# Retention and two feed-forward blocks: the moving operands of the four large products read as two interleaved halves

## The chip, the cores and the metric

The kernel runs on one core of a Trainium2 chip. The metric is the device time of one execution in microseconds (us). The engines are PE (TensorE: matmuls; its weight loads are listed as PEld), DVE (VectorE), ACT (ScalarE), POOL (GpSimd) and SP (SyncE, which issues the DMAs).

## The reference

```python
def _attn_ref(q, k, v):                       # (4, 8, 768, 64) each
    gamma = 1.0 - 2.0 ** (-5.0 - np.arange(H))
    for t in range(S):
        state = gamma * state + outer(k[:, :, t], v[:, :, t])
        y[:, :, t] = scale * (q[:, :, t] @ state)

def _moe_ref(x, w_in, w_out):                 # x (3072, 512), w_in (512, 2048), w_out (2048, 512)
    h = x @ w_in
    return np.maximum(0.01 * h, h) @ w_out

def _moe2_ref(x, w_in, w_out):
    h = x @ w_in
    return (h - np.tanh(h)) @ w_out

# reference: y as (3072, 512), then _moe_ref, then _moe2_ref
```

The four large products are the two matrix products of each feed-forward block. The weights of the blocks come in 64-bit floats, which the kernel turns into 32-bit ones itself.

## The kernel before

Tokens are worked on in six blocks (`nb`, `NC` = 6) of 512: four batches of 128 tokens each. In the feed-forward blocks a tile is 128 partitions by 512 words of 32 bits; for activations the partitions are features and the 512 words are tokens.

**Retention** (lines 368 to 566) leaves x as tiles `xw`, features by tokens.

**First product** (`product`, L637 to L645). The token blocks are taken in pairs and the 2x2 blocks of x and `w_in` are multiplied by a scheme of seven products (Strassen's, in Winograd's form), 8 groups of them for each of the three pairs of blocks: 168 products. Each operand was split into an upper and a lower part (`xch`, `xcl`, `wg`); a product is 2 halves of the contraction times 3 matmuls (upper x upper, upper x lower, lower x upper). The moving operand is x. The sums go through `collect` and `rectify` into tiles `c` and to memory as `g1s`, features by tokens.

**Second product** (`mm_out1`, L595 to L613). For each of 96 tiles (6 blocks by 16 feature tiles) the tile `gr` is read back, split into `gh` and `gl` (ACT, then DVE), and multiplied: 4 output tiles times 3 matmuls. The moving operand is g, the stationary one the weights `wo`. After 16 feature tiles, four ACT copies `st` (L611) take the sums out of PSUM, and DMAs write them to `x2s`. The sums alternate between PSUM banks 0 to 3 and 4 to 7 from block to block.

**Third product** (`mm_l1`, L755). For each of 96 tiles: 4 contraction tiles times 3 matmuls. The moving operand is the split `xkh`, `xkl` of what `x2s` holds; the stationary one is `w2h`, `w2l` of `w_in` (half 0 of `W2`).

**Fourth product** (`mm_l2`, L768). For each of 96 tiles: 4 token groups times 3 matmuls. Here the stationary operand is the activation (`gh`, `gl`), and the moving one is the weight (half 1 of `W2`), so that the output comes out as tokens by features, is copied out by `evac` and written to `out`.

The weights of the second block are split by `second_weights` (L741 to L753) while the second product still runs; `el_1` and `el_2` compute h - tanh(h) and split it between the third and the fourth product, which alternate, the third being two tiles ahead.

The order of the instructions is written out by hand, with small generators that run in the background by a budget of microseconds; no scheduler moves anything. In each of the four products a matmul names a moving operand of 512 words in a row. The helper `split` (L143) is an ACT copy that rounds to the upper part and a subtraction for the lower one.

Of the kernel before, what the change touches and what calls it, by code (L numbers as in the profile page):

```python
# [9 lines left out]
F32 = mybir.dt.float32  # L10
# [4 lines left out]
AF = mybir.ActivationFunctionType  # L15
ALU = mybir.AluOpType
# [8 lines left out]
NK = DM // P  # L25
NM = DFF // P
# [45 lines left out]
def kernel(  # L72
# [12 lines left out]
    nc = tc.nc  # L85
# [20 lines left out]
    def alloc(nm, dt=F32, shape=(P, TB)):  # L106
        pool, tag = free.popleft()
        serial[0] += 1
        t = pool.tile(list(shape), dt, tag=tag, name=f"{nm}_{serial[0]}")
        home[id(t)] = (t, pool, tag)  # L110
        return t

    def give(*ts):
        for t in ts:
            _, pool, tag = home.pop(id(t))
            free.append((pool, tag))
# [26 lines left out]
    def split(hi, lo, src, eng):  # L143

        nc.scalar.activation(out=hi, in_=src, func=AF.Copy)  # L145
        eng.tensor_tensor(out=lo, in0=src, in1=hi.bitcast(F32), op=ALU.subtract)  # L146

    def upper(hi, src, scale=None):
        if scale is None:
            nc.scalar.activation(out=hi, in_=src, func=AF.Copy)  # L150
        else:
            nc.scalar.activation(out=hi, in_=src, func=AF.Copy, scale=scale)
# [423 lines left out]
    def bank(i, nm):  # L576
        return mp.tile([P, TB], F32, tag=f"b{i}", name=nm)
# [9 lines left out]
    G, ACC = {}, {}  # L587
# [7 lines left out]
    def mm_out1(n):  # L595
        nb, m = divmod(n, NM)
        if m == 0:
            for j in range(4):
                ACC[j] = bank((nb + 1) % 2 * 4 + j, f"o1_{nb}_{j}")
        g, w = G.pop(n), WO[m]  # L600
        for j in range(4):
            c = slice(j * P, (j + 1) * P)
            for i, (a, b) in enumerate(((w[0][:, c], g[0]), (w[0][:, c], g[1]), (w[1][:, c], g[0]))):
                nc.tensor.matmul(ACC[j], a, b, start=m == 0 and i == 0, stop=m == NM - 1 and i == 2)  # L604
        give(*g)
        if nb == NC - 1:
            give(*WO.pop(m))
        if m == NM - 1:
            for j in range(4):
                st = alloc("st")  # L610
                nc.scalar.activation(out=st, in_=ACC[j], func=AF.Copy)  # L611
                nc.sync.dma_start(out=x2s[nb, j], in_=st)
                give(st)  # L613

# [22 lines left out]
    def product(sb, g, nm):  # L637
        an, bn, bk, _ = PROD[nm]
        ps, first = get_bank(sb, g, bk)
        a, b = WG[g][0][an], XC[sb][bn]  # L640
        for kt in range(2):
            c = slice(kt * P, (kt + 1) * P)
            for i, (w, x) in enumerate(((a[0], b[kt][0]), (a[0], b[kt][1]), (a[1], b[kt][0]))):
                nc.tensor.matmul(ps, w[:, c], x, start=first and kt == 0 and i == 0, stop=kt == 1 and i == 2,  # L644
                                 skip_group_check=True)  # L645

    KEPT = {}
# [40 lines left out]
    for i, (at_, sb, g, nm) in enumerate(stream):  # L688
# [13 lines left out]
        if xleft:  # L702
            c, p = xleft.pop(0)
# [30 lines left out]
    W2 = {}  # L734

    def reload_w2(m):
        rl = cm.tile([P, 2, DM], F32, tag="raw", name=f"w2r_{m}", bufs=RAW_BUFS)
        nc.sync.dma_start(out=rl, in_=w2s[m])
        return rl

    def second_weights():  # L741
        rl = {0: reload_w2(0), 1: reload_w2(1)}
        for m in range(NM):
            if m + 2 < NM:
                rl[m + 2] = reload_w2(m + 2)
            while len(free) < 8:
                yield None
            W2[m] = []
            for half in range(2):
                W2[m].append((alloc("w2h", F32R), alloc("w2l", F32R)))  # L750
                split(*W2[m][half], rl[m][:, half], nc.vector)
                yield 0.7
            rl.pop(m)  # L753

    def mm_l1(n):  # L755
        nb, m = divmod(n, NM)
        h = bank(4 + n % 4, f"h_{n}")
        w = W2[m][0]
        for kt in range(NK):
            x = xk[nb, kt]  # L760
            c = slice(kt * P, (kt + 1) * P)
            for i, (a, b) in enumerate(((w[0][:, c], x[0]), (w[0][:, c], x[1]), (w[1][:, c], x[0]))):
                nc.tensor.matmul(h, a, b, start=kt == 0 and i == 0, stop=kt == NK - 1 and i == 2)  # L763
            if m == NM - 1:
                give(*x)
        H[n] = h

    def mm_l2(n):  # L768
        nb, m = divmod(n, NM)
        if m == 0:  # L770
            for j in range(4):
                ACC[j] = bank(j, f"acc_{nb}_{j}")
        g, w = G.pop(n), W2[m][1]
        for j in range(4):
            c = slice(j * P, (j + 1) * P)
            for i, (a, b) in enumerate(((g[0][:, c], w[0]), (g[0][:, c], w[1]), (g[1][:, c], w[0]))):
                nc.tensor.matmul(ACC[j], a, b, start=m == 0 and i == 0, stop=m == NM - 1 and i == 2)  # L777
        give(*g)

    def evac(n):  # L780
# [37 lines left out]
    for n in range(NT):  # L818
# [10 lines left out]
        nb, m = divmod(n, NM)  # L829
# [18 lines left out]
    for n in range(-LAG, NT):  # L848
        n1 = n + LAG
        if n1 < NT:  # L850
            nb, m = divmod(n1, NM)
# [71 lines left out]
```

## Time and profile before

| | |
|---|---|
| median of 3 runs | 1138.69 us (1138.53 to 1138.78) |
| span of the profiled execution | 1136.7 us |
| PE busy | 1126.8 us (99%) |
| DVE, ACT, POOL busy | 753.2, 594.1, 169.5 us |
| PE weight loads | 932.5 us, beside the matmuls |

The span runs from the first to the last instruction of the program in the one execution that was profiled; for that execution nothing but the span is given, and the median of the timed runs is 2.0 us above it. A matmul's busy time holds its way through the array, and the next one begins before it ends; how fast PE goes is therefore read from the distance between starts, or from the number of matmuls in a stretch in which PE was busy without a break.

### The profile page before, as it was taken

The numbers are of one execution on the slowest core, as the hardware profiler recorded it, in microseconds if no ns is written. First come the engines' busy times: TensorE is split into PE (matmuls) and PEld (weight loads), VectorE is DVE, ScalarE is ACT, GpSimd is POOL, SyncE is SP. The second block draws the span as 40 slices with busy tenths as digits, with TensorE's granted clock in tenths as the row PEclk, the third lists the DMA queues.
The fourth block names the chain that finished last, engine by engine and source line by source line (L and its number), as shares of the span: only waits on it lengthen the run. The fifth ranks groups of instructions, "written<-read, shape, count | busy, mean of one in ns | idle before, by whom it ended". The sixth has DMA issues, their size and how long they took to land.

```text
span 1136.7 us, 16464 instructions
## 1 busy us (share of the span) xinstructions
PE 1126.8 (99%) x6075; PEld 932.5 (82%) x6075; DVE 753.2 (66%) x1264; ACT 594.1 (52%) x1025; POOL 169.5 (15%) x156
## 2 busy tenths in 40 slices
PE   9999999999999999999999999999999999999998
PEld 6888788888888888888888888888888888888886
DVE  3578897656778566364464667677667667677665
ACT  5766677546666324333454445445455445445443
POOL 3230000000000000000001232232232232232221
PEclk9999999999999999999999999999999999999999
DMA  9995555774668676476562002002001000100000
GB/s 233 251 248 167 203 187 186 253 248 156 233 232 296 234 266 241 171 273 229 203 244 74 1 1 74 1 1 73 2 1 50 25 1 29 47 1 6 32 1 37
DMA packets 134449, 148.03 MB, mean 130 GB/s; under 512 B 57440, under 2 KB 86240, under 8 KB 134368
## 3 DMA queue, kind: packets, MB, share of 16 engines
q1 hardware_dynamic: 134080, 146.83, 38.8%
q8 instruction: 47, 0.77, 0.3%
q14 instruction: 34, 0.28, 0.1%
q10 hardware_dynamic: 288, 0.15, 0.0%
HBM read 96.61 MB, written 50.33 MB: 129 GB/s over the span
## 4 chain that ended last, share of the span: by engine, by line
PE 96%; DVE 2%; issue 1%; ACT 1%; DMA 0%; SPq 0%; DVEq 0%; ACTq 0%
PE acc L777 23%; PE h L763 23%; PE o L604 23%; PE X L644 11%; PE Y L644 5%; PE Z L644 3%; PE sc L489 2%; PE y L511 2%; PE y L507 2%; PE kTp L454 1%; PE qTp L468 1%; PE u L528 1%; DMA k<-in_k_dram 0%; ACT c L633 0%; DVE c L657 0%
## 5 line engine op out<-in xcount | busy, mean ns | idle before, releaser
L146 POOL TENSOR_TENSOR gl<-e,gh 128x512 fp32r<-128x512 f32 x95 | 122.7, 1292 | 878.1 <-ACT gh L145 822.2
L604 PE MATMUL o<-gh,wo 128*128 128x512 f32 x768 | 237.1, 389 | 0.0
L145 ACT ACTIVATE gh<-e 128x512 fp32r<-128x512 f32 x96 | 60.7, 633 | 220.2 <-DVE e L804 220.2
L604 PEld LDWEIGHTS o<-gh,wo 128*128 128x128 f32 x768 | 144.2, 188 | 30.0
L797 DVE SCALAR_TENSOR_TENSOR e<-e,h 128x512 f32<-128x512 f32 x96 | 66.0, 687 | 152.4 <-ACT e L795 152.4
L777 PE MATMUL acc<-w2h,gl 128*128 128x512 f32 x384 | 149.6, 390 | 0.0
L604 PE MATMUL o<-gl,wo 128*128 128x512 f32 x384 | 149.5, 389 | 0.1
L777 PE MATMUL acc<-w2h,gh 128*128 128x512 f32 x384 | 149.4, 389 | 0.0
L777 PE MATMUL acc<-w2l,gh 128*128 128x512 f32 x384 | 149.4, 389 | 0.0
L763 PE MATMUL h<-xkh,w2h 128*128 128x512 f32 x384 | 149.4, 389 | 0.0
L763 PE MATMUL h<-xkl,w2h 128*128 128x512 f32 x384 | 149.4, 389 | 0.0
L763 PE MATMUL h<-xkh,w2l 128*128 128x512 f32 x384 | 149.4, 389 | 0.0
L146 DVE TENSOR_TENSOR gl<-gr,gh 128x512 fp32r<-128x512 f32 x96 | 64.6, 686 | 98.8 <-ACT gh L145 97.3
L644 PE MATMUL X<-xch,wg 128*128 128x512 f32 x384 | 126.7, 390 | 1.3 <-DVE wg L156 1.3
L644 PEld LDWEIGHTS X<-xch,wg 128*128 128x128 f32 x384 | 71.9, 188 | 17.3 <-DVE wg L156 2.2
L777 PEld LDWEIGHTS acc<-w2h,gl 128*128 128x128 f32 x384 | 72.0, 188 | 15.7 <-DVE gl L146 0.4
L604 PEld LDWEIGHTS o<-gl,wo 128*128 128x128 f32 x384 | 72.1, 188 | 15.2 <-DVE gl L146 0.5
L777 PEld LDWEIGHTS acc<-w2h,gh 128*128 128x128 f32 x384 | 72.1, 188 | 15.1 <-ACT gh L145 0.2
L763 PEld LDWEIGHTS h<-xkl,w2h 128*128 128x128 f32 x384 | 72.1, 188 | 15.0
L763 PEld LDWEIGHTS h<-xkh,w2l 128*128 128x128 f32 x384 | 72.1, 188 | 14.9
L777 PEld LDWEIGHTS acc<-w2l,gh 128*128 128x128 f32 x384 | 72.1, 188 | 15.0
L763 PEld LDWEIGHTS h<-xkh,w2h 128*128 128x128 f32 x384 | 72.0, 188 | 14.8
(89 smaller groups left out, 1856.7 us busy)
## 6 DMA issues: line engine op xcount, KB each, us to landing
g1s<-c SPq DMA_DIRECT2D x96, 256.0 KB, 2.1
gr<-g1s SPq DMA_DIRECT2D x96, 256.0 KB, 4.8
raw<-in_moe_w_in_dram SPq DMA_DIRECT2D x32, 512.0 KB, 5.4
raw<-in_moe_w_out_dram SPq DMA_DIRECT2D x32, 512.0 KB, 4.4
w2s<-cv SPq DMA_DIRECT2D x32, 256.0 KB, 4.4
w2r<-w2s SPq DMA_DIRECT2D x16, 512.0 KB, 5.8
q<-in_q_dram SPq DMA_DIRECT2D x24, 256.0 KB, 4.0
k<-in_k_dram SPq DMA_DIRECT2D x48, 128.0 KB, 3.8
```

The lines of the kernel that those rows point to most:

```text
L145: nc.scalar.activation(out=hi, in_=src, func=AF.Copy)
L146: eng.tensor_tensor(out=lo, in0=src, in1=hi.bitcast(F32), op=ALU.subtract)
L454: nc.tensor.transpose(ps[:, b, :], d["k"][:, b].rearrange("p h d -> p (h d)"), ident)
L468: nc.tensor.transpose(ps[:, b, e, :], d["qp"][:, b2 + b, e].rearrange("p h d -> p (h d)"), ident)
L489: nc.tensor.matmul(sc[h][:, b, :], d["kT"][r, b, :], d["qT"][r, b, tq], start=True, stop=True)
L507: nc.tensor.matmul(y[r, b, :], U[p][r, b, :], d["qT"][r, b, tq], start=b == 0, stop=False)
L511: nc.tensor.matmul(y[r, b, :], d["v"][:, b, h, :], d["A"][h][:, b, :], start=c == 0 and b == 0, stop=b == NB - 1)
L604: nc.tensor.matmul(ACC[j], a, b, start=m == 0 and i == 0, stop=m == NM - 1 and i == 2)
L644: nc.tensor.matmul(ps, w[:, c], x, start=first and kt == 0 and i == 0, stop=kt == 1 and i == 2, skip_group_check=True)
L763: nc.tensor.matmul(h, a, b, start=kt == 0 and i == 0, stop=kt == NK - 1 and i == 2)
L777: nc.tensor.matmul(ACC[j], a, b, start=m == 0 and i == 0, stop=m == NM - 1 and i == 2)
L797: nc.vector.scalar_tensor_tensor(out=w, in0=u, scalar=C3, in1=h, op0=ALU.mult, op1=ALU.mult)
```

## The change

A new helper `il` gives a view of a tile of 512 words in which word 2b + a is word 256a + b of the tile: 0, 256, 1, 257, and so on. All moving operands of the four products go through it. As two neighbouring words of the view are 256 words apart, a matmul now reads its moving operand in steps of 1024 bytes forth and 1020 bytes back.

Each of the first three products so turns the order of its tokens once; three such turns make word 8b + a (a below 8, b below 64) out of 64a + b in one direction, and the reverse in the other. The four copies `st` behind the second product, where two turns are done, now read PSUM in steps of 8 words and write in a row, which puts the order so that the third product's turn gives the tokens their places again. In the fourth product the moving operand is a weight, so its columns are turned beforehand: the split of half 1 in `second_weights` reads in steps of 2 words and writes in a row, on ACT and DVE as before.

Built, both programs have the same instructions in the same order on every engine and on the same tiles; the access patterns named here differ, and 22 matmuls get one wait more. These are the first matmuls into a PSUM bank: 15 of the second product in blocks 2 to 5, 3 of the third (tiles 0 to 2) and 4 of the fourth (tile 0). Each now also waits on PE's own counter, for the matmuls that used its bank before. In the changed kernel the lines behind the helper are 4 to 13 higher.

```diff
--- before.py
+++ after.py
@@ -144,6 +144,10 @@
 
         nc.scalar.activation(out=hi, in_=src, func=AF.Copy)
         eng.tensor_tensor(out=lo, in0=src, in1=hi.bitcast(F32), op=ALU.subtract)
+
+    def il(x):
+
+        return x.rearrange("p (a b) -> p b a", a=2)
 
     def upper(hi, src, scale=None):
         if scale is None:
@@ -601,14 +605,15 @@
         for j in range(4):
             c = slice(j * P, (j + 1) * P)
             for i, (a, b) in enumerate(((w[0][:, c], g[0]), (w[0][:, c], g[1]), (w[1][:, c], g[0]))):
-                nc.tensor.matmul(ACC[j], a, b, start=m == 0 and i == 0, stop=m == NM - 1 and i == 2)
+                nc.tensor.matmul(ACC[j], a, il(b), start=m == 0 and i == 0, stop=m == NM - 1 and i == 2)
         give(*g)
         if nb == NC - 1:
             give(*WO.pop(m))
         if m == NM - 1:
             for j in range(4):
                 st = alloc("st")
-                nc.scalar.activation(out=st, in_=ACC[j], func=AF.Copy)
+                nc.scalar.activation(out=st.rearrange("p (a b) -> p a b", a=8),
+                                     in_=ACC[j].rearrange("p (b a) -> p a b", a=8), func=AF.Copy)
                 nc.sync.dma_start(out=x2s[nb, j], in_=st)
                 give(st)
 
@@ -641,7 +646,7 @@
         for kt in range(2):
             c = slice(kt * P, (kt + 1) * P)
             for i, (w, x) in enumerate(((a[0], b[kt][0]), (a[0], b[kt][1]), (a[1], b[kt][0]))):
-                nc.tensor.matmul(ps, w[:, c], x, start=first and kt == 0 and i == 0, stop=kt == 1 and i == 2,
+                nc.tensor.matmul(ps, w[:, c], il(x), start=first and kt == 0 and i == 0, stop=kt == 1 and i == 2,
                                  skip_group_check=True)
 
     KEPT = {}
@@ -748,7 +753,15 @@
             W2[m] = []
             for half in range(2):
                 W2[m].append((alloc("w2h", F32R), alloc("w2l", F32R)))
-                split(*W2[m][half], rl[m][:, half], nc.vector)
+                hi, lo = W2[m][half]
+                if half == 0:
+                    split(hi, lo, rl[m][:, 0], nc.vector)
+                else:
+                    src = rl[m][:, 1].rearrange("p (b a) -> p a b", a=2)
+                    nc.scalar.activation(out=hi.rearrange("p (a b) -> p a b", a=2), in_=src, func=AF.Copy)
+                    nc.vector.tensor_tensor(out=lo.rearrange("p (a b) -> p a b", a=2), in0=src,
+                                            in1=hi.rearrange("p (a b) -> p a b", a=2).bitcast(F32),
+                                            op=ALU.subtract)
                 yield 0.7
             rl.pop(m)
 
@@ -760,7 +773,7 @@
             x = xk[nb, kt]
             c = slice(kt * P, (kt + 1) * P)
             for i, (a, b) in enumerate(((w[0][:, c], x[0]), (w[0][:, c], x[1]), (w[1][:, c], x[0]))):
-                nc.tensor.matmul(h, a, b, start=kt == 0 and i == 0, stop=kt == NK - 1 and i == 2)
+                nc.tensor.matmul(h, a, il(b), start=kt == 0 and i == 0, stop=kt == NK - 1 and i == 2)
             if m == NM - 1:
                 give(*x)
         H[n] = h
@@ -774,7 +787,7 @@
         for j in range(4):
             c = slice(j * P, (j + 1) * P)
             for i, (a, b) in enumerate(((g[0][:, c], w[0]), (g[0][:, c], w[1]), (g[1][:, c], w[0]))):
-                nc.tensor.matmul(ACC[j], a, b, start=m == 0 and i == 0, stop=m == NM - 1 and i == 2)
+                nc.tensor.matmul(ACC[j], a, il(b), start=m == 0 and i == 0, stop=m == NM - 1 and i == 2)
         give(*g)
 
     def evac(n):
```

## Rows read from the trace of the kernel before

**Rows 1.** The page: busy time and share of each engine; granted TensorE clock in 40 slices.
```profile
PE 1126.8 (99%) x6075; PEld 932.5 (82%) x6075; DVE 753.2 (66%) x1264; ACT 594.1 (52%) x1025; POOL 169.5 (15%) x156
...
PEclk9999999999999999999999999999999999999999
```
**Rows 2.** The page: the chain that ended last, by engine and by line.
```profile
PE 96%; DVE 2%; issue 1%; ACT 1%; DMA 0%; SPq 0%; DVEq 0%; ACTq 0%
PE acc L777 23%; PE h L763 23%; PE o L604 23%; PE X L644 11%; PE Y L644 5%; PE Z L644 3%; PE sc L489 2%; PE y L511 2%; PE y L507 2%; PE kTp L454 1%; PE qTp L468 1%; PE u L528 1%; DMA k<-in_k_dram 0%; ACT c L633 0%; DVE c L657 0%
```
**Rows 3.** Stretches of the first feed-forward's second product and of the second feed-forward.
```profile
core 0: us, PE busy (x) PEld busy (x) DVE busy (x) ACT busy (x) POOL busy (x), PEclk, DMA share, GB/s
400.00:590.00 190.00, 190.00 (x839) 157.36 (x839) 100.92 (x175) 77.84 (x134) 0.00 (x0) 1.00 0.66 240
625.00:1120.00 495.00, 495.00 (x2185) 410.02 (x2184) 346.65 (x557) 250.52 (x404) 133.44 (x101) 1.00 0.06 20
```
**Rows 4.** The page's groups: one of each of the four products, and its weight load.
```profile
L604 PE MATMUL o<-gh,wo 128*128 128x512 f32 x768 | 237.1, 389 | 0.0
...
L777 PE MATMUL acc<-w2h,gl 128*128 128x512 f32 x384 | 149.6, 390 | 0.0
...
L763 PE MATMUL h<-xkh,w2h 128*128 128x512 f32 x384 | 149.4, 389 | 0.0
...
L644 PE MATMUL X<-xch,wg 128*128 128x512 f32 x384 | 126.7, 390 | 1.3 <-DVE wg L156 1.3
...
L763 PEld LDWEIGHTS h<-xkh,w2h 128*128 128x128 f32 x384 | 72.0, 188 | 14.8
```
**Rows 5.** Time line of PE from 800 us: first and last of 19 matmuls (start, us).
```profile
799.73 0.39 PE L763 MATMUL h<-xkl,w2h 128*128 128x512 f32 x1
...
803.81 0.39 PE L777 MATMUL acc<-w2l,gh 128*128 128x512 f32 x1
```
**Rows 6.** Time line of PEld there: the first two weight loads.
```profile
799.96 0.19 PEld L763 LDWEIGHTS h<-xkh,w2h 128*128 128x128 f32 x1
800.18 0.19 PEld L763 LDWEIGHTS h<-xkl,w2h 128*128 128x128 f32 x1
```
**Rows 7.** Groups by form, whole span: ACT and DVE with and without a step in memory.
```profile
L146 DVE TENSOR_TENSOR gl<-gr,gh 128x512 fp32r<-128x512 f32 x96 | 64.6, 686 | 98.8 <-ACT gh L145 97.3 <-issue 1.4
...
L193 DVE SCALAR_TENSOR_TENSOR cv<-raw,cv 128x512 int32<-128x512 int32 x64 | 45.2, 706 | 1.9
...
L184 ACT ACTIVATE cv<-raw 128x512 f32<-128x512 f32 x64 | 42.2, 666 | 13.8 <-DMA raw<-in_moe_w_out_dram 7.3 <-DMA raw<-in_moe_w_in_dram 6.5
...
L150 ACT ACTIVATE xch<-xq_B 128x512 fp32r<-128x512 f32 x28 | 16.1, 623 | 0.1
...
L469 ACT ACTIVATE qT<-qTp 128x512 f32<-128x512 f32 x24 | 15.3, 639 | 4.1 <-PE qTp L468 4.1
...
L456 ACT ACTIVATE kT<-kTp 128x512 f32<-128x512 f32 x24 | 14.2, 593 | 7.6 <-PE kTp L454 7.5
```
**Rows 8.** Groups by form from 400 to 590 us: the copies that the change steps.
```profile
L146 DVE TENSOR_TENSOR w2l<-w2r,w2h 128x512 fp32r<-128x512 f32 x30 | 19.8, 687 | 6.1 <-ACT w2h L145 6.1
L145 ACT ACTIVATE w2h<-w2r 128x512 fp32r<-128x512 f32 x30 | 17.9, 623 | 8.6 <-DMA w2r<-w2s 5.8 <-PE o L604 2.8
...
L611 ACT ACTIVATE st<-o 128x512 f32<-128x512 f32 x16 | 9.6, 598 | 68.6 <-PE o L604 67.8
```
**Rows 9.** Time line of ACT where the second feed-forward begins.
```profile
613.59 2.06 ACT L611 ACTIVATE st<-o 128x512 f32<-128x512 f32 x4
615.50 1.28 ACT L145 ACTIVATE gh<-e 128x512 fp32r<-128x512 f32 x2
```
**Rows 10.** Time line of POOL there.
```profile
616.24 2.54 POOL L146 TENSOR_TENSOR gl<-e,gh 128x512 fp32r<-128x512 f32 x2 [522.63 <-ACT gh L145]
```
**Rows 11.** Waits from 614 to 619 us: in total, times, longest.
```profile
PEld acc L777 <- POOL gl L146: 0.4, 1, 0.4
```
**Rows 12.** Time line of PE there: the first matmuls of the fourth product.
```profile
614.03 0.39 PE L604 MATMUL o<-gh,wo 128*128 128x512 f32 x1
...
616.98 0.39 PE L777 MATMUL acc<-w2h,gh 128*128 128x512 f32 x1
617.21 0.39 PE L777 MATMUL acc<-w2l,gh 128*128 128x512 f32 x1
617.58 0.50 PE L777 MATMUL acc<-w2h,gl 128*128 128x512 f32 x1
617.92 0.40 PE L777 MATMUL acc<-w2h,gh 128*128 128x512 f32 x1
```

## The prediction

> **What bounds the kernel now.** I began with the page's busy times and then the chain of waits, to see whether any other engine stands in the way of the end. PE is busy 1126.8 of 1136.7 us, and the granted clock is at its upper level in every slice, 2.4 GHz [rows 1]; 96% of the chain is PE, and 88% are the lines of the four products: 23% each at L777, L763 and L604, 11 + 5 + 3 = 19% at L644 [rows 2]. Two stretches show that this is a bound and no average: from 400 to 590 us and from 625 to 1120 us PE is busy without a break, 190.00 of 190.00 and 495.00 of 495.00 us, with 839 and 2185 matmuls [rows 3]. That is 226.5 us per thousand, 0.2265 us each, in both, though DMA is at 0.66 in one and 0.06 in the other. The time line says the same: 18 distances from 799.73 to 803.81 us make 0.2267 us [rows 5]. At 2.4 GHz this is 544 clock periods for 512 moving columns: one a period and 32 more per matmul. A matmul's own row has 389 or 390 ns whichever product it is in [rows 4], so two are always in the array at once, and the next weight load (188 ns) begins when a matmul begins and is over before the next one [rows 4, 6]. So whatever is added to the distance between matmuls is added to the end; whatever only makes one start earlier or later is hidden by its neighbour.
>
> Counted from the loops, these matmuls are 96 x 12 = 1152 in each of the second, third and fourth product and 168 x 6 = 1008 in the first, 4464 in all. 4464 x 0.2267 = 1012 us, which is 89% of the span. Everything below is a price per matmul times 4464.
>
> **The change part by part.** No instruction is added, taken out or moved on any engine, and no DMA changes its place or its size. Four things differ.
>
> First, the moving read. All 4464 matmuls read 512 words alternately from two places 1024 bytes apart. No row of before shows PE reading out of sequence, so the price is bounded by the nearest rows. Below nothing: the 32 periods beyond one per column could shrink or go, since nothing in the rows says whether they belong to the weights or to the moving read; that is at most 13.3 ns a matmul, 4464 x 13.3 ns = -59.5 us. Above: the nearest rows of an engine that steps through memory are ACT's read of every second word, 666 ns for 512 words where a read in a row takes 623, ACT's write of every second word, 639 ns against 593 for the same kind of copy, and DVE's read of every second word, 706 against 686 ns [rows 7]. As prices they say 20 to 46 ns for 512 words. As rates they say only that words out of a row are delivered at one in 1.3 ns, and PE takes one in 0.42 ns. If PE got no more than ACT does, a matmul would take 666 ns instead of 226.7, and 4464 x 439 ns = +1961 us. Between these far ends I take the value that the rows as prices are nearest to: stepping cost the two engines 3 to 8% of an instruction that is not overlapped with its neighbour, and on PE the start of a matmul is covered by the one before. A start-up price of this kind does not show where two are in flight, so I take 0, and keep both ends.
>
> [...]
>
> Second, the 24 copies `st` read PSUM in steps of 8 words. They take 598 ns; the 16 in the stretch shown come after 67.8 us in which ACT sat idle [rows 8], and the banks that the first 20 empty are not written again for a block of 16 tiles, 16 x 12 x 0.2267 = 43.5 us. These cost nothing even at double the time. The last four are close to the path: they run from 613.59 for 2.06 us, behind them on ACT stand the two upper parts for the fourth product, behind these POOL's lower part, and PE waits 0.4 us for it [rows 9 to 11]. So their price goes to the end four times over. With the 46 ns of the nearest row it is 4 x 46 = 0.18 us; doubled copies would make 4 x 0.6 = 2.4 us. I take 0.2.
>
> Third, 16 ACT and 16 DVE instructions of the second half of the weights read in steps of two words. By the same rows they take 20 to 43 ns more each, 1 us in all. Nearly all stand before 590 us (30 of the 32 of both halves on each engine), where ACT is idle for 112 of 190 us and DVE for 89 [rows 3, 8], and the weights are wanted at 616.98 us, when the fourth product begins [rows 12]. Price 0; without this cover it would be that 1 us.
>
> Fourth, the 22 added waits of PE on itself. What they wait for is at least one tile of 12 matmuls back: the second product's last matmul starts at 614.03, the fourth product's first at 616.98 [rows 12]; in the other cases it is a block back. So the wait is over before it is asked. Behind a waiting matmul all of PE stands, so the price would be that of a restart: after the stall at 617.58 the next start comes 0.34 us later instead of 0.227, 0.11 us too much [rows 12]. 22 x 0.11 = 2.4 us is the upper end, 0 the lower and what I take.
>
> The sum for the profiled execution is 1136.7 + 0 + 0.2 + 0 + 0 = 1136.9 us. The median of the runs is 2.0 us above the span, so 1138.9 us. A measurement of this kernel can tell about 0.2%, 2.3 us, from no change, so this is "the same".
>
> **The rivals.** *Every column is a fetch of its own, at half the column rate.* Place: the moving read of each of the 4464 matmuls. [...] If a fetch takes two periods, a matmul has 1024 + 32 = 1056 periods, 440 ns, and 4464 x 213.3 ns = 952 us are added: 1138.7 + 952 = 2091 us. For it: the rows show stepped words only at 1.3 ns each and more, and a rate has no cover on PE, which is busy in 190.00 of 190.00 us. Against it: no engine here loses more than 8% by a step. It decides from 0.5 ns a matmul on, which is 2.3 us. [...]
>
> *A fixed surcharge per matmul that the neighbour does not cover.* With 20 to 46 ns as ACT and DVE pay, 4464 x 20 = 89 to 4464 x 46 = 205 us: 1228 to 1344 us. For it: the rows of ACT and DVE. Against it: the overlap of two matmuls.
>
> *The 32 periods go.* If they are a hitch of the moving read at each change of weights, two lines in turn may cover it: down to 1138.7 - 59.5 = 1079 us. For it: they come in every product alike and weight loads of 188 ns do not explain them. Against it: they are just as well the change of the weights in the array, which the order of the moving words does not touch.
>
> That the change does not do what it says can be left out: the access patterns of the built matmuls differ.
>
> **How the numbers follow.** No change 0.38; half the column rate 0.32; the fixed surcharge or another penalty short of half the rate 0.10; the 32 periods going in part or whole 0.17; worse than half the rate, up to 3100 us, 0.03. The two groups of cases stand on both sides of the forecast, so I give its own range first: 1136.5 to 1143.5, the upper end by the 2.4 us of the copies and the 2.4 us of the waits. The range of the forecast reaches to the rivals, from 1079 (all 32 periods) to 2110 (half the rate and 19 us for what else then turns late), and leaves 0.03 and little more out. Faster 0.17; the same 0.38; slower 0.32 + 0.10 + 0.03 = 0.45.
>
> **What would show it.** The distance between starts in the time line of PE at 800 us decides: 0.227 (mine), 0.44 (half the rate), 0.25 to 0.27 (surcharge), 0.213 (the 32 periods gone). The number of matmuls in an unbroken stretch of 190 us says the same: 839, 432, 700 to 770, 890. The copies `st` should stand near 0.64 us, the split of half 1 near 0.66 on ACT and 0.71 on DVE, and PE's wait for POOL's lower part at the start of the fourth product near 0.6 us. I am wrong if the distance differs from 226.7 ns by more than half a nanosecond, whatever the rest does.

## The result, and the profile after

The changed kernel takes 1095.95 us (median of 4 runs, 1095.91 to 1096.19), the kernel before 1138.68 (1138.53 to 1138.78). The ratio is 0.9625, 95% interval 0.9612 to 0.9639: 42.7 us or 3.75% faster. The forecast was no change; the time lies inside the stated range, on the side that was given 0.17.

PE is still what bounds it, with 47 us less to do. From the page of the changed kernel, the busy times and the chain, beside [rows 1, 2]. The profile follows this chain back only to 189 us, so its shares add up to 82%; in the first product a part of it now runs through DVE and ACT:

```profile
PE 1079.9 (99%) x6075; PEld 937.2 (86%) x6075; DVE 770.0 (70%) x1264; ACT 604.6 (55%) x1025; POOL 169.3 (15%) x156
...
PE 78%; DVE 2%; issue 1%; ACT 1%; DMA 0%; POOL 0%; DVEq 0%; POOLq 0%; ACTq 0%
```

The two stretches that are free of breaks again are so [rows 3], but hold more: 882 matmuls in 190.00 us and 2063 in 445.00, which is 0.2155 and 0.2157 us each.

```profile
core 0: us, PE busy (x) PEld busy (x) DVE busy (x) ACT busy (x) POOL busy (x), PEclk, DMA share, GB/s
400.00:590.00 190.00, 190.00 (x882) 166.36 (x882) 108.23 (x175) 86.75 (x138) 0.00 (x0) 1.00 0.63 228
625.00:1070.00 445.00, 445.00 (x2063) 389.67 (x2062) 328.54 (x526) 232.68 (x385) 126.23 (x96) 1.00 0.06 22
```

The time line of PE at 800 us says it directly [rows 5]: the first and the nineteenth matmul start 3.88 us apart, 18 distances of 0.2156 us, against 0.2267.

```profile
799.63 0.38 PE L776 MATMUL h<-xkh,w2l 128*128 128x512 f32 x1
...
803.51 0.38 PE L790 MATMUL acc<-w2h,gl 128*128 128x512 f32 x1
```

A period is here 0.4167 ns, taken for one column: an estimate from the first matmuls of both traces, eleven of 512 columns of 16-bit words each. In the kernel before nine distances between their starts, from 1.59 to 5.43 us, are 426.7 ns, 0.8333 ns a column; in the changed kernel the last two, from 4.45 to 4.88 us, are 217 and 215 ns, about half, and half of 0.8333 is 0.4167. The prediction's 2.4 GHz is the same figure as a rate; [rows 1] has the granted clock only in tenths. Counted so, a matmul of the four products went from 544 periods to 518: 512 columns and 6 instead of 32. The groups show it for every product alike [rows 4]. A matmul's row (mean ns behind the comma) fell from 389 to 379, and it is about 163 ns longer than the distance in both kernels; the weight load has stayed at 188 or 189.

```profile
L608 PE MATMUL o<-gh,wo 128*128 128x512 f32 x768 | 229.2, 379 | 0.0
...
L790 PE MATMUL acc<-w2h,gl 128*128 128x512 f32 x384 | 145.7, 380 | 0.3 <-POOL gl L146 0.3
...
L776 PE MATMUL h<-xkh,w2h 128*128 128x512 f32 x384 | 145.5, 379 | 0.0
...
L776 PEld LDWEIGHTS h<-xkh,w2h 128*128 128x128 f32 x384 | 72.6, 189 | 10.3
...
L649 PE MATMUL X<-xch,wg 128*128 128x512 f32 x384 | 123.3, 381 | 3.9 <-DVE wg L160 2.6 <-DVE c L662 1.2
```

4464 matmuls times 10.84 ns are 48.4 us; the span fell by 42.6, from 1136.7 to 1094.1. The first product is where the rest stayed. Its first and last matmul in the kernel before (last two numbers ahead of the forms), and then in the changed one:

```profile
L644 PE MATMUL X<-xch,wg x384: 387/389/504, 115.0 to 349.8; 128*128 128x512 f32 x192
```
```profile
L649 PE MATMUL X<-xch,wg x384: 379/379/483, 115.2 to 343.9; 128*128 128x512 f32 x192
```

234.8 us became 228.7: 6.1 gained where 1008 matmuls should give 10.9. From there to the last matmul, 1131.4 and 1089.0 us, 36.5 were gained of 37.3 (3444 matmuls, as 12 of the second product stand before the end of the first). The waits of PE's weight loads in the first product (in total, times, longest) are for tiles that DVE makes. First those of the kernel before, then the longest of the changed one, where the waits for `c` are new:

```profile
PEld X L644 <- DVE wg L156: 2.2, 2, 1.5
PEld Y L644 <- DVE xcl L156: 1.8, 1, 1.8
```
```profile
PEld X L649 <- DVE wg L160: 3.4, 2, 1.7
...
PEld X L649 <- DVE c L662: 3.3, 5, 0.8
...
PEld Y L649 <- DVE xcl L160: 2.1, 1, 2.1
```

Part of this is that others became slower. ACT and DVE read every second word of `raw` when they convert the weights. These instructions are as they were, yet take 853 and 823 ns on the mean where they took 666 and 706 [rows 7]. The split of the second half of the weights, which reads so only in the changed kernel, takes 868 and 836 ns; the copies `st`, which step through PSUM, stay at 599 [rows 8].

```profile
L188 ACT ACTIVATE cv<-raw 128x512 f32<-128x512 f32 x64 | 54.3, 853 | 15.2 <-DMA raw<-in_moe_w_in_dram 7.9 <-DMA raw<-in_moe_w_out_dram 7.1
...
L197 DVE SCALAR_TENSOR_TENSOR cv<-raw,cv 128x512 int32<-128x512 int32 x64 | 52.6, 823 | 1.9
...
L615 ACT ACTIVATE st<-o 128x512 f32<-128x512 f32 x24 | 14.0, 599 | 66.0 <-PE o L608 65.4
...
L761 ACT ACTIVATE w2h<-w2r 128x512 fp32r<-128x512 f32 x16 | 13.9, 868 | 0.5 <-PE o L608 0.5
...
L762 DVE TENSOR_TENSOR w2l<-w2r,w2h 128x512 fp32r<-128x512 f32 x16 | 13.4, 836 | 1.5 <-PE o L608 0.7 <-ACT w2h L761 0.6
```

### The profile page after: what moved, and what is told of

It is laid out like the page before. It is cut to its first block, busy times and chain, and to the rows that moved or that the text cites. A ratio compares the mean times of both kernels' runs of the same rounds, so it can differ in the third digit from the quotient of the medians.

```text
span 1094.1 us, 16468 instructions
## 1 busy us (share of the span) xinstructions
PE 1079.9 (99%) x6075; PEld 937.2 (86%) x6075; DVE 770.0 (70%) x1264; ACT 604.6 (55%) x1025; POOL 169.3 (15%) x156
## 4 chain that ended last, share of the span: by engine, by line
PE 78%; DVE 2%; issue 1%; ACT 1%; DMA 0%; POOL 0%; DVEq 0%; POOLq 0%; ACTq 0%
PE acc L790 23%; PE h L776 22%; PE o L608 22%; PE X L649 6%; PE Y L649 3%; PE Z L649 2%; DVE c L662 1%; DVE xcl L160 0%; ACT xch L154 0%; ACT c L638 0%; DVE xq_B L330 0%; DMA gr<-g1s 0%; DMA g1s<-c 0%; DVE gl L146 0%; POOL gl L146 0%
## 5 line engine op out<-in xcount | busy, mean ns | idle before, releaser
L608 PE MATMUL o<-gh,wo 128*128 128x512 f32 x768 | 229.2, 379 | 0.0
L790 PE MATMUL acc<-w2h,gl 128*128 128x512 f32 x384 | 145.7, 380 | 0.3 <-POOL gl L146 0.3
L608 PE MATMUL o<-gl,wo 128*128 128x512 f32 x384 | 145.7, 380 | 0.2 <-DVE gl L146 0.2
L790 PE MATMUL acc<-w2h,gh 128*128 128x512 f32 x384 | 145.6, 379 | 0.0
L776 PE MATMUL h<-xkh,w2h 128*128 128x512 f32 x384 | 145.5, 379 | 0.0
L776 PE MATMUL h<-xkl,w2h 128*128 128x512 f32 x384 | 145.5, 379 | 0.0
L776 PE MATMUL h<-xkh,w2l 128*128 128x512 f32 x384 | 145.5, 379 | 0.0
L790 PE MATMUL acc<-w2l,gh 128*128 128x512 f32 x384 | 145.5, 379 | 0.0
L649 PE MATMUL X<-xch,wg 128*128 128x512 f32 x384 | 123.3, 381 | 3.9 <-DVE wg L160 2.6
```

Of the source, the lines that this page charges most:

```text
L608: nc.tensor.matmul(ACC[j], a, il(b), start=m == 0 and i == 0, stop=m == NM - 1 and i == 2)
L649: nc.tensor.matmul(ps, w[:, c], il(x), start=first and kt == 0 and i == 0, stop=kt == 1 and i == 2, skip_group_check=True)
L776: nc.tensor.matmul(h, a, il(b), start=kt == 0 and i == 0, stop=kt == NK - 1 and i == 2)
L790: nc.tensor.matmul(ACC[j], a, il(b), start=m == 0 and i == 0, stop=m == NM - 1 and i == 2)
```

## The experiments

In the short diffs `b`, `x` are the moving and `a`, `w` the stationary operands; o is the second product (`mm_out1`), X the first, h the third and acc the fourth. Distances are medians of the differences between starts in the trace; the rows shown give them too, as mean ns less 163, or up to 182 less where the read is slow. All but the last two kernels are the kernel before with the matmuls edited in one or more products, a different edit in each, and ran once, beside the kernel before at 1138.65 to 1138.67 us; the orders of words that they read are not put right. Periods are those of 0.4167 ns estimated above. A line of a tile is here four words in a row, 16 bytes, a unit for telling the orders apart; how far the runs show its size stands at the end.

**Fewer moving columns.**

```diff
-                nc.tensor.matmul(h, a, b, start=...
+                n0 = TB if i != 1 else 256
+                nc.tensor.matmul(h[:, :n0], a, b[:, :n0], start=...
...
+                n0 = TB if i != 2 else 384
+                nc.tensor.matmul(ACC[j][:, :n0], a, b[:, :n0], start=...
```

> The kernel before, with moving operands in a row, but the second of three matmuls of the third product takes 256 of 512 columns and the third of three of the fourth product 384 (the left-out columns of these parts are missing from the sum). In the kernel before a matmul of 512 columns takes 544 periods, in the changed one 518; the question is what the 26 belong to. Theory F (a fixed loss per matmul, whether from the weights or from the start of the moving read): distance after the 256 columns 256 + 32 = 288 periods, 120.0 ns, after the 384 columns 416 periods, 173.3 ns. Theory M (the moving read in a row loses a period for every 20 words or so, 26 in 512): 256 + 6 + 13 = 275 periods, 114.6 ns, and 384 + 6 + 20 = 410, 170.8 ns. The full matmuls keep 226.7 ns under both.

```profile
L779 PE MATMUL acc<-w2h,gh 128*128 128x512 f32 x384 | 152.8, 398 | 8.1 <-ACT st L789 6.0 <-ACT gh L145 2.0
...
L764 PE MATMUL h<-xkh,w2h 128*128 128x512 f32 x384 | 152.4, 397 | 2.2 <-ACT xkh L145 2.2
...
L779 PE MATMUL acc<-w2h,gl 128*128 128x384 f32 x384 | 129.8, 338 | 1.0 <-POOL gl L146 1.0
```

After 256 columns the next start came at 117 ns (281 periods), after 384 at 174 (418), and the full matmuls beside them went up to 230 to 234. Neither theory gives that. The periods beyond the columns are 25 after 256, 34 after 384, and 40 to 50 after the full matmuls, for which both theories had 32. Inconclusive.

**Fewer weight columns in one matmul of three.**

```diff
-                nc.tensor.matmul(ACC[j], a, b, start=...
+                f = P if i != 1 else 64    # 32 in the fourth product
+                nc.tensor.matmul(ACC[j][:f], a[:, :f], b, start=...
```

> The kernel before, with moving operands in a row, but the second of three matmuls loads 64 of 128 weight columns in the second product and 32 in the fourth (the rows of the output that these leave out miss that part of the sum). Theory W (the 26 periods are lost to the reading of the next matmul's weights, 512 bytes a partition beside the moving words): the matmul during which the shorter weights are loaded loses 13 periods with 64 columns, distance 531 periods or 221.3 ns, and 6 or 7 with 32 columns, 524 to 525 periods or 218.5 ns; all others keep 226.7. Theory M (the moving read by itself) and theory S (a start-up of each moving read): 226.7 ns everywhere, the shorter loads change nothing.

```profile
L605 PE MATMUL o<-gh,wo 128*128 128x512 f32 x768 | 238.8, 391 | 0.0
...
L605 PEld LDWEIGHTS o<-gl,wo 128*64 128x64 f32 x384 | 51.5, 134 | 16.7 <-DVE gl L146 0.5
```

The shorter load is seen (134 ns instead of 188), but no distance fell: 227, 231 and 231 ns in the second product, 227.5, 233 and 230 in the fourth. The run took 1147.78 us. Against theory W, and not what M says either.

**Four ways of reading the moving operand.**

```diff
-                nc.tensor.matmul(ACC[j], a, b, ...          # o
+                nc.tensor.matmul(ACC[j], a, b.rearrange("p (a b) -> p b a", a=4), ...
-                nc.tensor.matmul(ps, w[:, c], x, ...        # X
+                nc.tensor.matmul(ps, w[:, c], x[:, :256].unsqueeze(1).broadcast_to([P, 2, 256]), ...
-                nc.tensor.matmul(h, a, b, ...               # h
+                nc.tensor.matmul(h, a, b.rearrange("p (b a) -> p a b", a=2), ...
-                nc.tensor.matmul(ACC[j], a, b, ...          # acc
+                nc.tensor.matmul(ACC[j], a, b.rearrange("p (a b c) -> p b a c", a=2, c=2), ...
```

> The kernel before with four ways of reading the moving operand, one per product, and nothing that puts the order right (token order and sums are not the reference's). First product: the first 256 words in a row, twice (two dimensions, but in a row). Second: four quarters read in turn (0, 128, 256, 384, 1, ...). Third: every second word, first the even then the odd ones. Fourth: two halves in turn by pairs (0, 1, 256, 257, 2, ...). If what helps is that neighbouring words come from lines far apart: 226.7, 216, 226.7 and 216 to 221 ns. If a view of two dimensions is enough: 216 in all four. If what helps is that each word needs a new line, pairs would give 226.7 and quarters 216. The slower reads of every second word by ACT and DVE (877 and 830 ns with the change, 660 and 691 before, in the first product) should come back to 660 and 691 there if the two reads in a row behave as before.

```profile
L604 PE MATMUL o<-gh,wo 128*128 128x512 f32 x768 | 282.7, 451 | 0.0
...
L763 PE MATMUL h<-xkh,w2h 128*128 128x512 f32 x384 | 242.9, 633 | 0.0
...
L777 PE MATMUL acc<-w2h,gh 128*128 128x512 f32 x384 | 196.5, 512 | 0.0
...
L644 PE MATMUL X<-xch,wg 128*128 128x512 f32 x384 | 126.8, 390 | 1.3 <-DVE wg L156 1.3
```

Distances: 226.7 ns for the first half twice, 283 for quarters, 451 for every second word, 335 for pairs. So a view of two dimensions does nothing by itself (226.7 ns), and "neighbouring words from far apart" is wrong as well: quarters are slower than a row, 283 ns. Every second word, at 451 ns, costs the half rate of the prediction's first rival.

**Four more.**

```diff
+                ... b.rearrange("p (d a b) -> p d b a", a=2, b=4)   # o
+                ... x.rearrange("p (a b c) -> p b a c", a=2, c=4)   # X
+                ... b.rearrange("p (a b c) -> p b a c", a=2, c=16)  # h
+                ... b.rearrange("p (b a) -> p a b", a=4)            # acc
```

> As the run with four ways of reading, with four others. First product: two halves in turn by whole 16-byte lines (0 to 3, 256 to 259, 4 to 7, ...). Second: neighbouring lines in turn, word by word (0, 4, 1, 5, 2, 6, 3, 7, 8, 12, ...). Third: two halves in turn by 64 bytes (0 to 15, 256 to 271, ...). Fourth: every fourth word (0, 4, 8, ..., 1, 5, ...), one word of each line at a time. If the distance in memory of the two streams is what helps: 216, 226.7, 216, 226.7 ns. If more time between fetches of new lines from one place is enough, 216 for the second as well. If each word's own line fetch (rather than two streams) is what changes the read: first and third 226.7, second and fourth 216. If a fetch per word has half the rate after all: fourth 440 ns.

```profile
L777 PE MATMUL acc<-w2h,gl 128*128 128x512 f32 x384 | 245.4, 639 | 0.0
...
L604 PE MATMUL o<-gh,wo 128*128 128x512 f32 x768 | 229.1, 379 | 0.0
...
L763 PE MATMUL h<-xkh,w2h 128*128 128x512 f32 x384 | 156.2, 407 | 0.0
...
L644 PE MATMUL X<-xch,wg 128*128 128x512 f32 x384 | 136.3, 416 | 0.7 <-DVE wg L156 0.7
```

216 ns for neighbouring lines in turn word by word, 246 to 254 for halves in turn by lines, 240 by 64 bytes, 460 for every fourth word. So what pays here is to take two lines in turn, word by word, and the lines may be neighbours (216 ns). A new line at every word is not enough: quarters (283 ns) and every fourth word (460 ns) have that too.

**A theory of two streams, tested on patterns chosen for it.** What puts all eight and the two kernels in order is to sort the sequence into its odd and its even places, called two streams here, and to count how many words each of them takes from a line before it leaves it. The streams are a way of counting; no trace shows what PE does inside a read, and theory P is no more than the author's estimate from these distances. The count does not give every size: P has half the rate for one word, and quarters and pairs, which are such orders too, took 283 and 335 ns.

```diff
+                ... b.rearrange("p (d a b) -> p d b a", a=2, b=64)  # o
+                ... x.rearrange("p (a b c) -> p c b a", a=2, c=2)   # X
+                ... b.rearrange("p (a b c) -> p c b a", a=2, c=4)   # h
+                ... b.rearrange("p (d a b) -> p d b a", a=2, b=2)   # acc
```

> The kernel before with four more ways of reading the moving operand and nothing that puts the order right (token order and sums are not the reference's). Theory P (the read works in pairs of columns: the first, third, fifth ... word of the sequence makes one stream, the second, fourth ... the other, and what counts is how many words a stream takes from a 16-byte line before it leaves it: four, no loss; two, as in a row, a little; one, half the rate). Theory D (neighbouring words must lie in different lines, nothing else counts). First product, halves in turn but every second word (0, 256, 2, 258, ...): two words of a line per stream, so P 540 to 610 periods, 225 to 254 ns; D 216. Second product, blocks of 64 in turn (0, 64, 1, 65, ...): both 216. Third, halves in turn but every fourth word (0, 256, 4, 260, ...): one word of a line per stream, P 440 to 460 ns, D 216. Fourth, pairs within a line (0, 2, 1, 3, 4, 6, 5, 7): P as in a row, 227; D more than 216, as all four words share a line. Also the slowing of ACT's and DVE's reads of every second word: if it needs two streams 1024 bytes apart, ACT 670 ns in the second product (256 bytes apart), 860 to 880 in the first.

```profile
L763 PE MATMUL h<-xkh,w2h 128*128 128x512 f32 x384 | 240.5, 626 | 0.0
...
L604 PE MATMUL o<-gh,wo 128*128 128x512 f32 x768 | 229.3, 379 | 0.0
...
L777 PE MATMUL acc<-w2h,gl 128*128 128x512 f32 x384 | 149.9, 390 | 0.0
...
L644 PE MATMUL X<-xch,wg 128*128 128x512 f32 x384 | 126.7, 390 | 1.3 <-DVE wg L156 1.3
```

216 (o), 226.7 (X), 451 (h) and 227 ns (acc): all four as P says; X and h speak against D. The last test of it was this:

```diff
+                ... b.rearrange("p (d a b) -> p d b a", a=2, b=8)      # o
+                ... x.rearrange("p (d a b) -> p d b a", a=2, b=16)     # X
+                ... b[:, :256].unsqueeze(2).broadcast_to([P, 256, 2])  # h
+                ... b.rearrange("p (d a b) -> p d b a", a=2, b=32)     # acc
```

> The kernel before with four more moving reads whose two streams take four words of each line, nothing put in order: first product, blocks of 16 in turn (streams 64 bytes apart); second, blocks of 8 (32 bytes); fourth, blocks of 32 (128 bytes); third, each of the first 256 words twice (both streams in the same line). Theory P (four words of a line per stream, wherever the streams are) gives 215.8 ns in all four. If the streams must be in different lines, the third gives 227 or more. For ACT's and DVE's reads of every second word, which 256 and 1024 bytes slow to 880 ns and more and 16 bytes leave at 671: if it is nearness that spares them, 660 to 671 in the second product (32 bytes) and between that and 880 in the first (64 bytes).

```profile
L763 PE MATMUL h<-xkh,w2h 128*128 128x512 f32 x384 | 145.5, 379 | 0.0
...
L644 PE MATMUL X<-xch,wg 128*128 128x512 f32 x384 | 123.1, 381 | 2.8 <-DVE wg L156 2.0 <-DVE c L657 0.8
```

215.8 ns in all four, also with both streams in one line. With nothing but the moving reads edited this run took 1093.34 us. Put together (with jumps: the stream goes to the other half between two of its lines; returning: it goes back to a line that it has left):

| sequence of words | words per line and visit of a stream | distance, ns | periods |
|---|---|---|---|
| in turn from two blocks of 256, 64, 32, 16, 8 or 4 words; each word twice | 4 | 216 | 518 |
| in a row; first half twice; 0, 256, 2, 258; 0, 2, 1, 3 | 2 | 227 | 544 |
| two halves in turn by 64 bytes; by 16 bytes | 2, with jumps | 240; 246 to 254 | 576; 590 to 610 |
| quarters in turn; pairs from two halves | 1, returning | 283; 335 | 680; 804 |
| every second word; halves, every fourth; every fourth | 1 | 451; 451; 460 | 1082; 1082; 1104 |

**The weights' part.** Three runs asked whether the 26 periods are lost to the weight load.

```diff
-            ... ((w[0][:, c], g[0]), (w[0][:, c], g[1]), (w[1][:, c], g[0]))        # o
+            ... ((w[0][:, j::4], g[0]), (w[0][:, j::4], g[1]), (w[1][:, j::4], g[0]))
+            ... w[0][:, kt % 2:256:2] ...                                          # h
+            ... g[0][:, j::4], and b.rearrange("p (a b) -> p b a", a=2)            # acc
+            ... w[:, kt::2],   and x.rearrange("p (a b) -> p b a", a=2)            # X
```

> The kernel before with the stationary operand read in steps (the output features are in another order and the sums are not the reference's): second product weights in steps of 4 words, moving operand in a row; third product weights in steps of 2, moving in a row; fourth weights in steps of 4 and first in steps of 2, both with the moving operand as two halves in turn. Theory M (the loss is the moving read's own): 227, 227, 216, 216 ns, as long as a weight load still fits beside a matmul. Theory W (the loss comes from weight words and moving words being read side by side): the distance moves with the way the weights are read, to 235 ns or more with a line per word in the second product, and above 216 in the fourth and first.

```profile
L604 PEld LDWEIGHTS o<-gh,wo 128*128 128x128 f32 x768 | 209.4, 310 | 0.1
...
L763 PE MATMUL h<-xkh,w2h 128*128 128x512 f32 x384 | 151.6, 395 | 0.0
...
L644 PE MATMUL X<-xch,wg 128*128 128x512 f32 x384 | 123.2, 381 | 3.7 <-DVE wg L156 2.4 <-DVE c L657 1.2
...
L763 PEld LDWEIGHTS h<-xkh,w2h 128*128 128x128 f32 x384 | 76.4, 199 | 11.1
```

With steps of 4 words a weight load takes 310 to 333 ns, longer than the distance. There o came to 232 to 237 ns and acc, with its halves in turn, to 235 to 237, above 216 as W has it; but a load of that length may set the pace by itself, so these two decide nothing. With steps of 2 it takes 193 to 199 and still fits: beside a row the distance is 233 ns instead of 227, beside two halves in turn 216 as without the steps. So that dearer weight read is felt beside a row and not beside the change's order.

```diff
-                nc.tensor.matmul(ACC[j], a, b, ...
+                nc.tensor.matmul(ACC[j][:64], a[:, :64], b, ...      # 32 in the fourth product
```

> The kernel before, with moving operands in a row, but every matmul of the second product takes 64 weight columns and every one of the fourth 32 (the other output rows are set to zero). Theory W (a matmul loses periods because the next matmul's weights are read while the moving operand is read in a row): 64 words are half of the reads, so 544 - 13 = 531 periods, 221 ns, in the second product, and 32 words 524 to 525 periods, 218.5 ns, in the fourth. Theory M (the moving read in a row is itself too slow by 26 periods): 226.7 ns in both.

```profile
L604 PE MATMUL o<-gh,wo 128*64 128x512 f32 x768 | 240.6, 393 | 0.0
...
L778 PE MATMUL acc<-w2h,gl 128*32 128x512 f32 x384 | 151.3, 394 | 0.1
```

```diff
-                nc.tensor.matmul(ACC[j], a, b, ...
+                nc.tensor.matmul(ACC[j], a[:, :1].broadcast_to([P, P]), b, ...
```

> The kernel before with stationary operands made of one word a partition, repeated for all 128 columns (outputs are not the reference's): in the second and third product with the moving operand in a row, in the fourth with four quarters read in turn. Theory W (weight lines and moving lines read side by side cost the 26 periods): one word is one line, so the loss goes, 216 to 217 ns in the second and third product. Theory M: 226.7 ns. Theory C (128 weight words cost their reads one by one, whether from one line or many): 226.7 ns too, and only fewer columns would help. Fourth product: 283 ns, as in the second product with four quarters, if those 162 periods are the moving read's own.

```profile
L604 PE MATMUL o<-gh,wo 128*128 128x512 f32 x768 | 240.9, 394 | 0.0
```

Neither half nor a quarter of the weight columns (230 to 232 ns), nor all weights from one line (231 to 233), took any of the loss away; the fourth product there, with quarters, kept its 283 ns. Theory W as stated is wrong, and so is C, as fewer columns did not help: the 26 periods go with the order of the moving read. But M does not hold to the letter either. Beside a row these changes of the weights moved the distance up, mostly by 3 to 6 ns, and in the run with fewer columns the third product, which was left as it was, moved too (226 to 231). How the two reads meet is open.

**The copies that put the order right.**

```diff
-                nc.scalar.activation(out=st.rearrange("p (a b) -> p a b", a=8),
-                                     in_=ACC[j].rearrange("p (b a) -> p a b", a=8), func=AF.Copy)
+                nc.scalar.activation(out=st, in_=ACC[j], func=AF.Copy)
...
+                split(*W2[m][half], rl[m][:, half], nc.vector)
```

> The changed kernel without what puts the order right: the copies behind the second product and the split of the second half of the weights read in a row again (tokens and output columns come out in another order). The prediction priced these at 0 to 5 us, most likely 0.2. Theory: they stay hidden, so 1095.7 to 1096.0 us, no difference. Rival: the slower stepped copies (868 and 836 ns where 620 and 690 would do) delay the second product, and without them the time falls by 1 us or more.

1095.93 us (1095.80 to 1096.03, 4 runs; ratio to before 0.9625, 0.961 to 0.9639). They cost nothing.

**Groups of 8: the better version.**

```diff
-        return x.rearrange("p (a b) -> p b a", a=2)
+        return x.rearrange("p (d a b) -> p d b a", a=2, b=4)
...
-                nc.scalar.activation(out=st.rearrange("p (a b) -> p a b", a=8),
-                                     in_=ACC[j].rearrange("p (b a) -> p a b", a=8), func=AF.Copy)
+                nc.scalar.activation(out=st, in_=ACC[j], func=AF.Copy)
...
-                    src = rl[m][:, 1].rearrange("p (b a) -> p a b", a=2)
+                    src = rl[m][:, 1].rearrange("p (d b a) -> p d a b", a=2, b=4)
```

> The changed kernel with another order of reading: in each group of 8 words the two neighbouring 16-byte lines in turn (0, 4, 1, 5, 2, 6, 3, 7). Three such turns give the order back, so the copies behind the second product read in a row again, and only the weights' second half is put in order in its split. Theory: 215.8 ns a matmul as in the changed kernel, and without the slowing of ACT's and DVE's reads of every second word (671 and 690 ns instead of 880 and 830), so that the first product waits less: of the 5.7 us by which the changed kernel misses 4464 x 10.83 = 48.4 us, 3 to 5 come back, 1091 to 1093 us. Rival: the lost 5.7 us are PE having caught up with the work that feeds it, whatever its reads do to others: 1095 to 1096 us.

1093.41 us (1093.24 to 1093.58, 4 runs), ratio 0.9603 (0.9587 to 0.9619). The kernel with plain copies, run in turn with it on the same chip, had no run under 1095.80, so this one beats both kernels. The matmuls are at 379 again, and the reads of every second word back at 668 ns:

```profile
L608 PE MATMUL o<-gh,wo 128*128 128x512 f32 x768 | 229.0, 379 | 0.0
...
L188 ACT ACTIVATE cv<-raw 128x512 f32<-128x512 f32 x64 | 42.3, 668 | 17.2 <-DMA raw<-in_moe_w_in_dram 9.6 <-DMA raw<-in_moe_w_out_dram 7.6
```

Its first product is 226.3 us long (115.2 to 341.6) against 228.7:

```profile
L648 PE MATMUL X<-xch,wg x384: 379/379/483, 115.2 to 341.6; 128*128 128x512 f32 x192
```

So 2.4 of the 4.8 us lost there go with the slowed conversions. The run with blocks of 16, 8 and 32 words, whose conversions were at 673 ns in the first product, agrees: its first product is 226.3 us long as well. The other 2.4 stayed, and PE's weight loads still wait there for tiles from DVE; that PE has caught up with what feeds it, as the rival said of all of it, was not tried by itself. The expected 1091 to 1093 us was a little too low: 2.5 us came back, not 3 to 5.

## Why the prediction was wrong

**What bounds the kernel** was right in the main: a price per matmul times 4464, with nothing on the path to cover it. What is added to the distance is added to the end, but not all that is taken off it came back: 42.6 of 48.4 us, mostly because the first product waits longer for DVE.

**"First, the moving read"** is the step that failed. It took 0, and the runs show -10.84 ns a matmul, -48.4 us, inside its lower end of -13.3 ns and -59.5 us. The distance at 800 us moved by 11 ns where half a nanosecond was the sign of being wrong. The reasons given were that the rows of ACT and DVE as prices are nearest, and that the start of a matmul is covered by the one before. Those rows are about engines that take a word in 1.2 ns and more, and neither reason touches the 32 periods, which are part of the distance itself while two matmuls are in flight. That the trace had 226.7 ns, by the estimate above 544 periods for 512 columns, in every product alike was the strongest fact in it, and the prediction left open whether they belong to the weights or to the moving read. Of the 32 periods 26 went, in all four products, with the order of the moving read. The rival that was given 0.17 had the size, but its reason, a hitch at each change of the weights, is not shown: the runs tie the loss to the order of the words.

**The half rate** was given 0.32, and exists: 451 ns a matmul for every second word, near the 440 worked out. The change's order, at 215.8 ns, is not one of those that pay it. The reason given for the rival, a fetch for every column, is not shown by any run. Nor is it the change of line from word to word that costs: counted along the sequence, every second word takes two words running from a line and has 451 ns, while halves in turn never take two running and have 216. Counted by streams, one word a line and visit costs most, 283 to 460 ns.

**The fixed surcharge** did not show with the change's order; other orders, at 240 to 335 ns, cost 13 to 108 ns more than a row without being at half rate (table above). The 20 ns of DVE was no price of a step either: the 706 of [rows 7] is a mean over all stages, and from 150 to 335 us of the kernel before DVE's two reads of every second word took 690 and 691 ns where a read in a row takes 686.

**The copies** were priced at 0.2 us, and the kernel with plain copies shows no difference. They did not slow at all (2.06 us for the last four, as in [rows 9]):

```profile
595.47 2.06 ACT L615 ACTIVATE st<-o 128x512 f32<-128x512 f32 x4
```

PE's stop at POOL's lower part grew: the start at 599.45 comes 0.63 us after the one before instead of 0.37 [rows 12]. The copies are not the reason, as the kernel with plain copies has the same 0.63; counted from the start of the second product's last matmul, PE comes to the fourth product after 2.81 us instead of 2.95, and POOL begins after 2.32 instead of 2.21 [rows 10, 12].

```profile
598.82 0.38 PE L790 MATMUL acc<-w2l,gh 128*128 128x512 f32 x1
...
599.45 0.48 PE L790 MATMUL acc<-w2h,gl 128*128 128x512 f32 x1 [0.25 <-POOL gl L146]
...
599.77 0.38 PE L790 MATMUL acc<-w2h,gh 128*128 128x512 f32 x1
```

**The weights' second half** was forecast at 0.66 us on ACT and 0.71 on DVE and took 0.868 and 0.836; the cover held. **The added waits** cost at most 0.8 us, which is all that was lost behind the first product, the longer stop at POOL's lower part included.

## What to carry to other kernels

When PE is busy without a break, hold the distance between matmul starts against the columns times the shortest time of a column that the trace itself gives: an unexplained remainder that is the same everywhere (here 13.3 of 226.7 ns, with the 0.4167 ns estimated above) is a price to be hunted, and worth a run that changes only access patterns. For the 32-bit moving operands here, a read that takes two neighbouring blocks of four words in turn, word by word, saved 4.8% a matmul (226.7 to 215.8 ns); in groups of 8 words it undoes itself after three products and left ACT's and DVE's reads of every second word as fast as before (668 and 698 ns, against 666 and 706). A moving operand read by every second or every fourth word doubled the time of a matmul here (451 and 460 ns), so an order that must be changed is better changed in a copy off the path: those of the change cost nothing (1095.95 us with them, 1095.93 without).

## What the runs showed of the hardware that was not expected

The distance of a matmul with 512 moving words went from 216 to 460 ns with their order alone, and in the 18 orders of the table, eight of them foretold, it goes with the number of words that each of the two streams takes from a line at a visit. That a line of 16 bytes is the one to count by shows in the blocks. With 8 bytes, blocks of 4 words in turn and blocks of 2 would count alike, and they took 216 and 227 ns; with 32 bytes, a row and blocks of 4 would, and they took 227 and 216. That is a way of counting 18 distances: no trace shows the streams or the lines themselves, and why one word a visit takes 283 ns in one order and 460 in another is open.

With the order of the moving read the time of another engine changed. ACT's read of every second word takes 658 to 680 ns beside a row, beside turns of lines 16, 32 and 64 bytes apart, and beside quarters; it takes 860 to 899 beside turns 256 and 1024 bytes apart and beside halves in turn by lines, while reads in a row (`c<-c`, 625 ns) stay as they are with the change. Here are the rows from 400 to 580 us, in the second product, beside blocks of 64 words in turn, which are 256 bytes apart, and beside blocks of 8, 32 bytes apart:

```profile
L184 ACT ACTIVATE cv<-raw 128x512 f32<-128x512 f32 x16 | 14.4, 899 | 11.3 <-DMA raw<-in_moe_w_out_dram 6.7 <-DMA raw<-in_moe_w_in_dram 4.5
```
```profile
L184 ACT ACTIVATE cv<-raw 128x512 f32<-128x512 f32 x15 | 10.2, 680 | 10.4 <-DMA raw<-in_moe_w_out_dram 6.8 <-DMA raw<-in_moe_w_in_dram 3.6
```

How far the two streams are apart is not the whole condition: 0, 256, 2, 258 at 227 ns is 1024 bytes apart too and left ACT at 658. What the condition is stays open.
